# The matmuls of the MLP read their moving operand from two interleaved runs instead of one

## The chip, the cores and the metric

The kernel runs on one core of a Trainium2 chip. The metric is the device time of one execution in microseconds; a profiled execution also gives its span, from the first to the last recorded instruction.

## The reference

Attention with a sigmoid in place of the softmax, for 8 batches of 12 heads, 448 tokens and 64 columns a head, and then an MLP over all 3584 tokens:

```python
scores = scale * q @ k.T - log(S)
attn = sigmoid(scores) @ v            # (8, 12, 448, 64)
x = attn -> (3584 tokens, 768)
h = x @ w_in                          # 768 x 2048
g = relu(h) ** 2
out = g @ w_out                       # 2048 x 768
```

The weights arrive as 64-bit floats and are turned into 32-bit ones on the chip.

## The kernel before

The program has two parts. The first is attention with the preparation of the weights; it runs to about 246 us of the span. The second is the MLP, which works through four groups of tokens, `GROUPS`: three of 1024 tokens (T = 512, twice) and a last one of 512 (T = 256, twice). For each group `gemm1` computes the hidden layer and `gemm2` the output. Both use a block scheme with 7 products in place of 8, over halves of the tokens, of the features and of the weights.

Accuracy comes from splitting. Every 32-bit operand `raw` is split by `split_to` into a high part `hi`, which ScalarE (ACT) writes with a cast to fp32r, and a low part `lo = raw - hi`, which VectorE (DVE) writes. `product` then issues three matmuls for each pair of blocks: high by high, high by low, low by high. The stationary operand `a[:, c]` is a 128 x 128 block of weights, the moving operand `b` a block of T token columns; in the last group's `gemm2` it is the other way round and the moving operand is 384 weight columns wide. TensorE writes each product into one PSUM bank, and sums over blocks there.

In `gemm1`, `run(n, i)` makes product n for weight block i: 3 blocks `c` times 3 passes, so 9 matmuls; 7 products and 8 values of i give 504 matmuls of 512 columns for each of the first three groups. In `gemm2` 7 products, 8 values of i, 3 output blocks e and 3 passes give 504 again. So six stages of 504 matmuls, 3024 in all, have a moving operand of 512 columns (`NS`). In the last group, `gemm1` has operands of 256 columns and some joined ones of 512 columns (`joined_product`, lines 614 and 616), and `gemm2` those of 384.

The moving operands of `gemm1` are made in `x_operands` by `make`: for each of 7 products one call of `split_to` for two blocks together (128 x 1024) and one for the third (128 x 512). Those of `gemm2` are made in `operand_of` by `split`, 28 calls a group of 128 x 1024 each (tiles `o_0h` to `o_3h` and `o_0l` to `o_3l`). The weights are split by `halve_weights`, which calls `split_to` as well (tiles `w`, `w1A` to `w1D`).

The steps of a group follow an order written out by hand (`REST`, and for the first group `LEAD` ahead of it); the `work` lists say behind which step an operand is loaded or split, and parts of the kernel run under `manual_schedule`, in program order. DMAs are issued from SyncE (SP). Attention multiplies plain F32 operands where it forms sums with v (lines 337 and 349): there four matmuls on 64 x 64 tiles of the array stand in a row, two on either half of the partitions, which read two different column runs of the same tile `at`.

Strided access exists already in the preparation of the weights: `convert_upper` (line 158, ACT) and `convert_join` (line 169, DVE) read every second 32-bit word of a tile of 64-bit words, and line 161 (ACT) reads and writes every second word.

Of the kernel before, what the change touches and what calls it, by code (L numbers as in the profile page):

```python
# [30 lines left out]
NS = 512  # L31
# [49 lines left out]
def sigmoid_attention_relu2_mlp(  # L81
# [51 lines left out]
    def op2(name, dtype=F32, n=S):  # L133
        return sb.tile([P, 2, n], dtype, tag="op2", bufs=N2, name=name)

    def op1(name, dtype=F32, n=S):
        return sb.tile([P, n], dtype, tag="op1", bufs=N1, name=name)
# [132 lines left out]
    def raw_of(half, k):  # L270
        if (half, k) not in raw_first:
            raw_first[half, k] = op2(f"x0_{half}{k}", n=NS), op1(f"y0_{half}{k}", n=NS)
        return raw_first[half, k]
# [98 lines left out]
    def split_to(hi, lo, raw, later=None):  # L372
        nc.scalar.copy(out=hi, in_=raw)  # L373
        if later is None:
            nc.vector.tensor_sub(out=lo, in0=raw, in1=hi.bitcast(F32))  # L375
        else:
            later.append(lambda: nc.vector.tensor_sub(out=lo, in0=raw, in1=hi.bitcast(F32)))

    def split(raw, name, new):
        hi, lo = new(name + "h", F32R), new(name + "l", F32R)  # L380
        split_to(hi, lo, raw)
        return hi, lo

    def x_operands(g):

        raw = {}
        t0, T = GROUPS[g]

        def load(n, b, k):
            if g == 0:
                raw[n] = raw_of(b, k)
                return
            r2, r1 = op2(f"x{n}_{g}", n=T), op1(f"y{n}_{g}", n=T)
            src = xd[3 * k : 3 * k + 3, :, t0 + b * T : t0 + (b + 1) * T].rearrange("c p s -> p c s")
            nc.sync.dma_start(out=r2, in_=src[:, 0:2])
            nc.sync.dma_start(out=r1, in_=src[:, 2])
            raw[n] = [r2, r1]

        def sub(n, a, b):
            for o, x, y in zip(raw[n], raw[a], raw[b]):
                nc.vector.tensor_sub(out=o, in0=x, in1=y)

        ops, ys = {}, {}

        def make(product, n, later=None, whole=False):
            if 2 * T > NS:
                y = op2(f"y{n}_{g}", F32R, T)
                h1, l1 = y[:, 0], y[:, 1]  # L410
                h2, l2 = (op2(f"{c}{n}_{g}", F32R, T) for c in ("xh", "xl"))
                ops[product] = [(h2[:, c], l2[:, c], None) for c in range(2)] + [(h1, l1, None)]
            else:
                x = op2(f"xj{n}_{g}", F32R, 2 * T)
                kind, at = SPOT[product]
                if kind not in ys:
                    ys[kind] = op2(f"yj{kind}_{g}", F32R, 2 * T)
                y = ys[kind][:, at]
                (h2, l2), (h1, l1) = ((t[..., :T], t[..., T:]) for t in (x, y))
                ops[product] = [(h2[:, c], l2[:, c], x[:, c]) for c in range(2)] + [(h1, l1, y)]  # L420
            (x2, x1) = raw[n]
            split_to(h2, l2, x2, later)
            if whole:
                later.append(lambda: split_to(h1, l1, x1))
            else:
                split_to(h1, l1, x1, later)

        load("11", 0, 0)
        load("12", 1, 0)
        load("22", 1, 1)  # L430
        load("21", 0, 1)
        raw["t2"] = raw["22"] if g == 0 else [op2(f"xt_{g}", n=T), op1(f"yt_{g}", n=T)]
        raw["t1"], raw["t3"], raw["t4"] = raw["12"], raw["11"], raw["21"]
        return ops, {
            1: lambda *later: make(1, "11", *later),
            2: lambda *later: make(2, "21", *later),
            "t1": lambda: sub("t1", "12", "11"),
            "t2": lambda: sub("t2", "22", "t1"),
            6: lambda *later: make(6, "t2", *later),
            "t3": lambda: sub("t3", "t2", "11"),  # L440
            7: lambda: make(7, "t3"),
            5: lambda: make(5, "t1"),
            3: lambda *later: make(3, "22", *later),
            "t4": lambda: sub("t4", "21", "t2"),
            4: lambda: make(4, "t4"),
        }
# [5 lines left out]
    last = len(pairs) - 1  # L452
    todo = [(m, i) for m in range(2) for i in range(NI) if m == 0 or i not in DEFERRED]
    x, vt, xs, at, pav, xo, f64, w = {}, {}, {}, {}, {}, {}, {}, {}
    ready, stores, later, words = [], [], [], []
# [119 lines left out]
    first = {}  # L575
# [28 lines left out]
    def product(out, w, c, x, first, last):  # L604
        (wh, wl), (xh, xl) = w, x
        for n, (a, b) in enumerate(((wh, xh), (wh, xl), (wl, xh))):
            nc.tensor.matmul(  # L607
                out, a[:, c], b, start=first and n == 0, stop=last and n == 2, skip_group_check=True
            )

    def joined_product(out, w, xs, first):
# [8 lines left out]
    def operand_of(g, raw, name, later=None):  # L620
        T = GROUPS[g][1]
        if 2 * T > NS:
            return (*split(raw, name, lambda *names: op2(*names, T)), None)
        both = op2(name, F32R, 2 * T)
        hi, lo = both[:, :, :T], both[:, :, T:]
        split_to(hi, lo, raw, later)
        return hi, lo, both

    def gemm1(g, ops, weights, between):
# [53 lines left out]
        def run(n, i):  # L683
# [10 lines left out]
            if n in joined:  # L694
                joined_product(out, w, ops[n], n in (1, 7, 2))
            else:
                for c in range(NE):
                    product(out, w, c, ops[n][c][:2], n in (1, 7, 2) and c == 0, c == NE - 1)
# [107 lines left out]
    def gemm2(g, blocks, operands1, weights1, ahead):  # L806
# [50 lines left out]
        for at, n in enumerate(order):  # L857
# [6 lines left out]
            with ExitStack() as fixed:  # L864
                if g == NG - 1 and n == 1:
                    fixed.enter_context(tc.manual_schedule())
                for j in range(NI // 2):
                    if at + 1 < len(order):
                        operand(order[at + 1], j)
                    if n in (4, 3):  # L870
                        ahead((n == 3) * NI // 2 + j)
                    for e in range(parts):
                        for i in (2 * j, 2 * j + 1):
                            w, x = (tuple(t[:, i % 2] for t in of[:2]) for of in (weights[n][j], ops[n][j]))
                            still, moving = (x, w) if turned else (w, x)
                            still = tuple(t.rearrange("p (c m) -> p c m", m=P) for t in still)
                            product(banks[k, e], still, e, moving, n in (1, 7, 2) and i == 0, i == NI - 1)
# [124 lines left out]
```

## Time and profile before

| | |
|---|---|
| median of 3 runs | 1055.15 us (1054.49 to 1055.74) |
| profiled execution, its own time | 1054.99 us |
| its span | 1053.2 us |
| TensorE busy | 1049.0 us, 100% of the span |
| VectorE busy | 802.9 us, 76% |
| ScalarE busy | 657.9 us, 62% |
| mean granted TensorE clock | 1.000 |

The profiled execution spends 1.8 us outside its span. The busy time of TensorE is that of its pipelined matmuls: one matmul is listed with the time from its start to its modelled end, longer than the time after which the next one starts. The pace is read from the chain of work, which lists how many matmuls follow one another in how many microseconds.

### The profile page before, as it was taken

The numbers are of one execution on the slowest core, as the hardware profiler recorded it, in microseconds if no ns is written. First come the engines' busy times: TensorE is split into PE (matmuls) and PEld (weight loads), VectorE is DVE, ScalarE is ACT, GpSimd is POOL, SyncE is SP. The second block draws the span as 40 slices with busy tenths as digits, with TensorE's granted clock in tenths as the row PEclk, the third lists the DMA queues.
The fourth block names the chain that finished last, engine by engine and source line by source line (L and its number), as shares of the span: only waits on it lengthen the run. The fifth ranks groups of instructions, "written<-read, shape, count | busy, mean of one in ns | idle before, by whom it ended". The sixth has DMA issues, their size and how long they took to land.

```text
span 1053.2 us, 16201 instructions
## 1 busy us (share of the span) xinstructions
PE 1049.0 (100%) x6194; PEld 818.3 (78%) x6194; DVE 802.9 (76%) x1024; ACT 657.9 (62%) x917; POOL 72.4 (7%) x42
## 2 busy tenths in 40 slices
PE   9999999999999999999999999999999999999998
PEld 4555555557888888888888888888888888899998
DVE  5999999996777698954555899655555998549994
ACT  7989989986765765634343757344333766248863
POOL 1322232210121000000000000000000000000000
PEclk9999999999999999999999999999999999999999
DMA  9988999964565336544333446442333344557464
GB/s 359 401 296 314 378 388 323 380 239 141 193 217 163 110 109 193 165 132 122 91 90 90 120 128 197 147 151 78 103 98 105 105 142 143 182 172 236 130 189 127
DMA packets 90366, 196.11 MB, mean 186 GB/s; under 512 B 8240, under 2 KB 51504, under 8 KB 90288
## 3 DMA queue, kind: packets, MB, share of 16 engines
q1 hardware_dynamic: 90288, 195.07, 55.9%
q8 instruction: 49, 0.80, 0.3%
q14 instruction: 29, 0.24, 0.1%
HBM read 154.14 MB, written 40.89 MB: 185 GB/s over the span
## 4 chain that ended last, share of the span: by engine, by line
PE 100%; ACT 0%; issue 0%
PE ha L607 22%; PE oa L607 22%; PE ob L607 11%; PE pav L337 11%; PE hb L607 9%; PE sc L305 9%; PE oc L607 5%; PE hc L607 5%; PE sr L322 2%; PE pav L349 2%; PE hb L614 1%; PE hb L616 1%; PE hc L614 1%; PE warm_ps L907 0%; PE hc L616 0%; ACT o L848 0%
## 5 line engine op out<-in xcount | busy, mean ns | idle before, releaser
L373 ACT CAST w<-w 128x768 fp32r<-128x768 f32 x108 | 89.4, 836 | 94.8 <-DMA w<-w 91.5
L375 DVE TENSOR_TENSOR w<-w 128x768 fp32r<-128x768 f32 x108 | 103.0, 956 | 29.3 <-ACT w L373 29.2
L676 ACT COPY s<-ha 128x512 f32<-128x512 f32 (+1 forms) x96 | 51.2, 533 | 118.4 <-PE ha L607 114.3
L290 ACT ACTIVATE at<-sc 128x896 f32<-128x896 f32 x144 | 119.3, 942 | 4.0 <-PE sc L305 3.9
L337 PE MATMUL pav<-at,v 64*64 64x448 f32 x1152 | 118.1, 540 | 0.0
L337 PEld LDWEIGHTS pav<-at,v 64*64 64x64 f32 x1152 | 41.6, 133 | 60.8 <-issue 53.9
L559 DVE TENSOR_TENSOR ql<-x,qh 128x896 fp32r<-128x896 f32 x47 | 72.4, 1581 | 0.0
L172 POOL TENSOR_TENSOR a<-a,f 128x768 int32<-128x768 int32 x26 | 58.2, 2237 | 159.8 <-DVE a L169 89.3
L679 DVE TENSOR_TENSOR g<-hb,s 128x512 f32<-128x512 f32 (+1 forms) x64 | 39.7, 620 | 32.4 <-ACT s L676 25.5
L375 DVE TENSOR_TENSOR w1A<-w1A 128x768 fp32r<-128x768 f32 x24 | 23.0, 957 | 53.6 <-ACT w1A L373 53.4
L305 PE MATMUL sc<-qh 64*128 64x448 f32 x282 | 53.7, 380 | 0.0
L305 PE MATMUL sc<-ql,qh 64*128 64x448 f32 x282 | 51.4, 361 | 0.0
L305 PE MATMUL sc<-qh,ql 64*128 64x448 f32 x282 | 51.4, 361 | 0.0
L373 ACT CAST w1A<-w1A 128x768 fp32r<-128x768 f32 x32 | 26.7, 835 | 32.7 <-DMA w1A<-w 30.0
L607 PE MATMUL oa<-o_0h,w 128*128 128x512 f32 x144 | 46.3, 389 | 0.0
L607 PE MATMUL oa<-o_1h,w 128*128 128x512 f32 x144 | 46.3, 389 | 0.0
L607 PE MATMUL oa<-o_2h,w 128*128 128x512 f32 x144 | 46.3, 389 | 0.0
L607 PE MATMUL oa<-o_3h,w 128*128 128x512 f32 x144 | 46.3, 389 | 0.0
L305 PEld LDWEIGHTS sc<-qh 64*128 64x128 f32 x282 | 26.4, 184 | 18.9 <-PE pav L337 16.2
L659 DVE SCALAR_TENSOR_TENSOR g<-g 128x1024 f32<-128x1024 f32 (+1 forms) x34 | 38.5, 1131 | 1.1
L373 ACT CAST w1C<-w1C 128x768 fp32r<-128x768 f32 x31 | 25.9, 834 | 20.4 <-DMA w1C<-w 20.4
L375 DVE TENSOR_TENSOR w1B<-w1B 128x768 fp32r<-128x768 f32 x23 | 23.0, 1001 | 19.9 <-ACT w1B L373 19.9
(315 smaller groups left out, 2764.8 us busy)
## 6 DMA issues: line engine op xcount, KB each, us to landing
w<-w SPq DMA_DIRECT2D x108, 384.0 KB, 3.3
x<-qk SPq DMA_DIRECT2D x47, 448.0 KB, 6.9
f<-w_in SPq DMA_DIRECT2D x16, 768.0 KB, 8.7
w1A<-w SPq DMA_DIRECT2D x32, 384.0 KB, 3.1
w1B<-w SPq DMA_DIRECT2D x31, 384.0 KB, 3.1
w1C<-w SPq DMA_DIRECT2D x31, 384.0 KB, 3.1
v<-v SPq DMA_DIRECT2D x24, 448.0 KB, 7.7
w<-s SPq DMA_DIRECT2D x26, 384.0 KB, 8.8
```

The lines of the kernel that those rows point to most:

```text
L172: nc.gpsimd.tensor_tensor(out=wb, in0=wb, in1=t.bitcast(I32)[:, :, 0], op=ALU.add)
L290: nc.scalar.activation(at, sc, AF.Sigmoid, bias=NEG_LOG_S, scale=SCALE)
L305: nc.tensor.matmul(sc[t][:, j], x[kp][rows, 1, ks], x[qp][rows, 0], start=(n == 0), stop=(n == len(passes) - 1),)
L322: nc.tensor.matmul(sc[r * KR : (r + 1) * KR, j], x[rows, 1, NT * P :], x[rows, 0], start=True, stop=True)
L337: nc.tensor.matmul(sums[columns, h], vt[rows, n % 2 * NT + t, columns], at[t][rows, j], start=(t == 0 and (n % 2, h) != (1, 1)), stop=(t = ...
L373: nc.scalar.copy(out=hi, in_=raw)
L375: nc.vector.tensor_sub(out=lo, in0=raw, in1=hi.bitcast(F32))
L559: nc.vector.tensor_sub(out=xs[n][1], in0=x[n], in1=xs[n][0].bitcast(F32))
L607: nc.tensor.matmul(out, a[:, c], b, start=first and n == 0, stop=last and n == 2, skip_group_check=True)
L659: nc.vector.scalar_tensor_tensor(out=t, in0=t, scalar=0.0, in1=t, op0=ALU.max, op1=ALU.mult)
L676: nc.scalar.copy(out=s, in_=banks["a", i])
L679: nc.vector.tensor_add(out=to, in0=from_[:, :T], in1=s)
```

## The change

The low and high parts of the moving operands of 512 columns are stored in another order: in each block of 512 tokens the 256 even tokens first, and the 256 odd ones behind them. The casts and subtractions that make these parts read `raw` with a step of two elements (8 bytes) and write the two runs one after the other, through a view with two rows. In `product` a moving operand of 512 columns is read through a view of 256 by 2: even token 0, odd token 0, even token 1, and so on, 1024 bytes to and fro. The order of the columns in the result is as before. The weights, the joined operands and the operands of the last group keep their layout. No instruction is added or removed.

```diff
+    def unwoven(t, order):
+        a = "a " if len(t.shape) > 2 else ""
+        return t.rearrange(f"p {a}({order}) -> p {a}n s", n=2)
+
+    def weave_to(hi, lo, raw, later=None):
+        split_to(unwoven(hi, "n s"), unwoven(lo, "n s"), unwoven(raw, "s n"), later)
+
+    def woven(t):
+        return t.rearrange("p (n s) -> p s n", n=2)
+
     def split(raw, name, new):
         hi, lo = new(name + "h", F32R), new(name + "l", F32R)
-        split_to(hi, lo, raw)
+        weave_to(hi, lo, raw)
         return hi, lo
...
-            split_to(h2, l2, x2, later)
+            to = weave_to if 2 * T > NS else split_to
+            to(h2, l2, x2, later)
             if whole:
-                later.append(lambda: split_to(h1, l1, x1))
+                later.append(lambda: to(h1, l1, x1))
             else:
-                split_to(h1, l1, x1, later)
+                to(h1, l1, x1, later)
...
         for n, (a, b) in enumerate(((wh, xh), (wh, xl), (wl, xh))):
+            moving = woven(b) if b.shape[-1] == NS else b
             nc.tensor.matmul(
-                out, a[:, c], b, start=first and n == 0, stop=last and n == 2, skip_group_check=True
+                out, a[:, c], moving, start=first and n == 0, stop=last and n == 2, skip_group_check=True
             )
```

## Rows read from the trace of the kernel before

**Rows 1.** The page: busy time of TensorE, and its clock in 40 slices.

```profile
PE 1049.0 (100%) x6194; PEld 818.3 (78%) x6194; DVE 802.9 (76%) x1024; ACT 657.9 (62%) x917; POOL 72.4 (7%) x42
...
PEclk9999999999999999999999999999999999999999
```

**Rows 2.** Waits of TensorE: all that the trace shows.

```profile
PE warm_ps L907 <- PEq L988: 0.8, 1, 0.8
```

**Rows 3.** Busy times by stage: attention, six stages of 504 matmuls, the last group.

```profile
core 0: us, PE busy (x) PEld busy (x) DVE busy (x) ACT busy (x) POOL busy (x), PEclk, DMA share, GB/s
0.00:246.32 246.32, 245.55 (x2404) 136.41 (x2405) 221.78 (x301) 216.46 (x280) 58.37 (x30) 1.00 0.90 333
246.32:360.50 114.18, 114.18 (x505) 94.51 (x504) 78.94 (x119) 73.15 (x114) 14.05 (x12) 1.00 0.54 172
...
817.50:931.77 114.27, 114.27 (x507) 94.62 (x506) 91.31 (x103) 64.05 (x84) 0.00 (x0) 1.00 0.47 144
931.77:1053.20 121.43, 117.99 (x768) 114.54 (x767) 97.62 (x160) 78.42 (x140) 0.00 (x0) 1.00 0.56 172
```

**Rows 4.** Chain of work: start, us, matmuls of 512, 256 and 384 columns.

```profile
376.82 16.32 PE oc L607 x72
...
943.48 2.16 PE ha L607 x18
...
999.84 8.32 PE oc L607 x48
```

**Rows 5.** Chain of work in attention: F32 operands of 448 columns, 64 x 64 tiles.

```profile
12.73 0.75 PE pav L349 x8
13.48 2.25 PE pav L337 x24
```

**Rows 6.** Groups of TensorE instructions: the same F32 matmuls, with their count.

```profile
L337 PE MATMUL pav<-at,v 64*64 64x448 f32 x1152 | 118.1, 540 | 0.0
```

**Rows 7.** Groups of ACT by shape: L373 reads in order, L158 every second word.

```profile
L373 ACT CAST w<-w 128x768 fp32r<-128x768 f32 x108 | 89.4, 836 | 94.8 <-DMA w<-w 91.5 <-PE oa L607 3.1
L158 ACT ACTIVATE a<-f 128x768 f32<-128x768 f32 x26 | 25.1, 964 | 0.0
...
L373 ACT CAST w1D<-w1D 128x384 fp32r<-128x384 f32 x32 | 16.4, 513 | 1.6 <-DMA w1D<-w 1.6
...
L158 ACT ACTIVATE b<-fd 128x384 f32<-128x384 f32 x12 | 6.7, 556 | 0.0
```

**Rows 8.** Groups of DVE by shape: L375 reads in order, L169 every second word.

```profile
L375 DVE TENSOR_TENSOR w<-w 128x768 fp32r<-128x768 f32 x108 | 103.0, 956 | 29.3 <-ACT w L373 29.2
...
L169 DVE SCALAR_TENSOR_TENSOR a<-f,a 128x768 int32<-128x768 int32 x26 | 24.9, 959 | 0.9
```

**Rows 9.** Timeline, second group: making o_2 and its first use by TensorE.

```profile
591.55 1.05 ACT L373 CAST o_2h<-g 128x1024 fp32r<-128x1024 f32 x1
...
594.97 1.22 DVE L375 TENSOR_TENSOR o_2l<-g,o_2h 128x1024 fp32r<-128x1024 f32 x1
...
597.24 0.39 PE L607 MATMUL oa<-o_2l,w 128*128 128x512 f32 x1
```

**Rows 10.** Busy times in the first product of the first group's second stage.

```profile
360.50:376.82 16.32, 16.32 (x74) 13.51 (x73) 16.31 (x17) 15.55 (x20) 0.00 (x0) 1.00 0.36 110
```

## The prediction

> **What bounds the kernel now.** The page first: TensorE is busy for 1049.0 of 1053.2 us, at full granted clock in all 40 slices [rows 1]. A busy TensorE can still wait, so the waits come next: in the whole trace TensorE waits once, 0.8 us at the start [rows 2]. Then the stages: six of 504 matmuls take 114.2 to 114.3 us each, busy for the whole stage, clock 1.00 [rows 3]. So whatever one of these matmuls costs more or less goes into the end time with the factor 3024, and what happens on ACT and DVE counts only if TensorE comes to wait for it.
>
> What such a matmul costs is read from the chain of work. 72 matmuls of 512 columns take 16.32 us, so 226.7 ns each; 48 of 384 columns take 8.32 us, so 173.3 ns; 18 of 256 columns take 2.16 us, so 120.0 ns [rows 4]. At 2.4 GHz, the upper of the clock's two levels, which a granted clock of 1.00 is, these are 544, 416 and 288 cycles: the columns plus 32 each time. Read in order, the moving operand therefore comes at one column a cycle, with no cycle lost that grows with its length. All six stages have this pace (504 by 226.7 ns is 114.2 us), so the reads meet nothing that disturbs them. A new read order can win nothing but those 32 cycles.
>
> **The change part by part.**
>
> *The read order.* No instruction is added. What changes is how 3024 matmuls fetch 512 columns: neighbours in the stream were neighbours in memory, 4 bytes apart; now each lies 1024 bytes from the one before. No matmul of this kernel reads like that, so I bound the price. Below: one column a cycle as today, 0 ns; a gain is limited to the 32 cycles, 13.3 ns. Above, the slowest stream of columns here is that of plain F32 operands in attention: 24 instructions of 448 columns take 2.25 us [rows 5], and as four tiles of the array run side by side (front: four matmuls on 64 x 64 tiles stand in a row), a set of four takes 375 ns or 900 cycles, 2.0 cycles a column. The code makes 576 calls at that line and the page counts 1152 instructions [rows 6], so a whole F32 matmul comes to 4.0 cycles a column. My bounds are thus 1 and 4 cycles a column, with a row at 2.0 between them.
>
> I take 2 cycles a column. A fp32r stream moves 4 bytes a cycle at 2.4 GHz on every partition, and the simplest way to hold that rate is to fetch several neighbours in one access. If it is done that way, the smallest such unit is a pair, and the new order breaks every pair: two accesses where there was one. That is an estimate from the bounds; no row shows the size of the unit. The sum: 2 by 512 plus 32 are 1056 cycles, 440.0 ns, 213.3 ns more than today; by 3024 it is 645.1 us. At 4 cycles a column it is 2080 cycles, 866.7 ns, 640.0 ns more and 1935 us in all.
>
> There is a rule that speaks against this read order in words. The Trainium skill, page SBUF — State Buffer (section "Door 1: The DMA port swizzle"), says that SBUF has 16-byte lines, that at least two consecutive accesses must fall on one line for full bandwidth, and that each step to a new line pays a penalty. In the old order four fp32 columns share a line, in the new one none do, so by that rule all 3024 matmuls slow down, by an amount that the page does not give; without it they stay at 226.7 ns. The trace before agrees in part: ACT, reading every second word, so two to a line, takes 964 ns in place of 836 for 768 elements [rows 7], where the rule would have it free, and DVE pays nothing [rows 8].
>
> *The casts on ACT.* A group has 7 products of two casts in its first stage and 28 casts in its second, 42; three groups have 126, of 1024 or 512 elements, which now read with a step of 8 bytes. The nearest rows: 964 against 836 ns for 768 elements, 556 against 513 for 384 [rows 7] (line 158 is another function, so part of it may not be the step). That is 0.11 to 0.17 ns an element, so 0.12 to 0.17 us for a cast of 1024, and no more than 21 us over the MLP, while ACT is idle for 41 to 50 us in the first and last of these stages alone [rows 3]. The cover for a single cast: o_2h ends at 592.60 and the subtraction behind it starts at 594.97 [rows 9], 2.4 us later. I cost it at nothing. If the cover were gone, each of the 126 would cost at most its 0.17 us.
>
> *The subtractions on DVE.* Also 126, with one input at a step of 8 bytes. Line 169, with such an input, takes 959 ns for 768 elements, the plain subtraction 956 [rows 8]. So nothing, and that matters: DVE is busy for 16.31 of 16.32 us where it is fullest [rows 10], and o_2l is written 1.05 us ahead of its first reader [rows 9]. 0.2 us more for each would eat that lead after five operands, and TensorE would wait. Were TensorE slower, both engines would gain time.
>
> *Everything else.* The writes stay runs of 256 elements, the loads are untouched, attention's 246 us and the last group's 121 us [rows 3] have no woven matmul. Each sum starts from the profiled execution, 1054.99 us (1053.2 of span and 1.8 around it), 0.16 us below the median of the runs, 1055.15. 1055.0 + 645.1 = 1700.
>
> **The rivals.**
>
> *The order of reads is free* (not slower; the change then does nothing to the time). Place: the fetch of a moving operand. If the memory serves any 4 bytes a cycle, the pace stays 544 cycles, and the time 1055. For it: the four tiles of attention read two different runs of one tile from the same partitions, 448 columns each in 375 ns [rows 5], so 896 elements in 900 cycles from two places, if they run side by side as the pace says. Against it: those may be two streams, each in order, and not one that jumps; and ACT's reads do feel a step [rows 7]. It decides as soon as one stream may jump every cycle without loss.
>
> *A mild penalty.* If jumping costs TensorE what a step costs ACT, 8 to 15% of the time [rows 7], a matmul takes 19 to 35 ns more, and 3024 of them 58 to 105 us: 1113 to 1160. For it: it is the only price of a stride in the trace. Against it: a step of two words leaves neighbours closer than a jump of 1024 bytes.
>
> *Four cycles a column or near it*: 1055 + 1935 = 2990. It comes if a fetch brings four columns and each jump loses three. For it: F32 operands run at that rate in sum [rows 5, 6]. Against it: there the rate comes from two instructions, not from the fetch.
>
> *A gain.* If part of the 32 cycles belongs to opening one run and two runs hide it, at most 13.3 ns by 3024, 40 us: 1015. Nothing in the trace ties them to the read order; they are the same for 256, 384 and 512 columns.
>
> **How the numbers follow.** Half rate 0.36; free 0.31; a mild penalty, with all between it and half rate, 0.13; beyond half rate 0.13; a gain 0.07. The likeliest gives the time, 1700; its own range is 1690 to 1745 (up to 2.07 cycles a column, 15 ns a matmul or 45 us in all; a little below for a pace not quite at 2). The range that leaves out the gain and everything beyond half rate, 0.20 together, is 1050 to 1745; it is wide because cases of both signs hold most of the chance. A measurement of this kernel can tell about 0.2% from no change: faster 0.07, same 0.31, slower 0.62.
>
> **What would show it.** The chain of work of the stage that starts near 360 us: 72 matmuls in 31.7 us for half rate, 16.3 if reads are free, 17.7 to 18.8 for the mild case, 62.4 at four cycles. The matmuls of 256 and 384 columns keep 120.0 and 173.3 ns in every case. ACT's casts of 1024 should go from 1.05 to about 1.2 us, DVE's subtractions stay at 1.22; under half rate both should show more idle time, waiting for TensorE. The prediction is wrong if the pace stays at 226.7 ns, or if TensorE shows waits for o_l or xl tiles. A granted clock below 1.00 in these stages would be a cost that I have not put in.

## The result and the profile after

The changed kernel takes 1026.88 us (median of 4 runs, 1026.30 to 1027.27) against 1054.86 for the kernel before beside it: ratio 0.9733, 95% interval 0.9716 to 0.975. It is 28 us faster, where 645 us more were forecast. The span went from 1053.2 to 1025.5 us.

The page shows less TensorE time and more on ACT and DVE, to set beside [rows 1]:

```profile
PE 1018.4 (99%) x6194; PEld 821.8 (80%) x6194; DVE 834.4 (81%) x1024; ACT 711.3 (69%) x917; POOL 72.3 (7%) x42
```

The pace is in the chain of work (start, us, what):

```profile
372.17 15.54 PE oc L619 x72
...
980.38 8.32 PE oa L619 x48
```

72 matmuls of 512 columns take 15.54 us in place of 16.32 [rows 4]: 215.8 ns or 518 cycles each, columns plus 6 in place of columns plus 32. The matmuls of 384 columns, which the change leaves alone, keep their 8.32 us for 48. 3024 by 10.8 ns are 32.8 us, but the span lost only 27.7. The busy times by stage show where the other 5 went:

```profile
246.34:356.42 110.08, 109.39 (x505) 95.29 (x506) 81.21 (x120) 78.72 (x112) 13.96 (x12) 1.00 0.57 178
...
465.41:575.87 110.46, 109.42 (x505) 95.01 (x505) 64.76 (x75) 51.76 (x76) 0.00 (x0) 1.00 0.37 109
575.87:684.65 108.78, 108.78 (x506) 95.26 (x505) 103.01 (x98) 77.76 (x76) 0.00 (x0) 1.00 0.48 151
```

The columns are those of [rows 3]. 504 by 215.8 ns are 108.78 us: the second stage of a group keeps that, the first stages take 1.3 to 1.8 us more, and TensorE is idle in them, which it was not before. Its waits are these (engine, us in total, times, longest):

```profile
PE ha L619 <- ACT s L688: 2.2, 3, 0.8
...
PE hb L619 <- DVE w1D L375: 0.6, 2, 0.3
```

The larger wait comes once in each first stage: TensorE waits for `s`, a copy of its sums out of PSUM, which stands on ACT behind casts of tokens. In the second group these took 1.56 us (xh) and 0.81 (y) in place of 1.05 and 0.62. The smaller wait comes at the end of the second and the third first stage, as the chain of work there shows:

```profile
567.56 1.96 PE ha L619 x9
...
570.02 1.58 ACT o_0h L373
571.60 0.42 ACT w1D L373
...
572.03 1.55 DVE o_0l L375
573.58 0.47 DVE w1D L375
...
574.10 1.78 PE hb L619 x7
```

TensorE's last product of the stage waits for w1D's low part, which stands on DVE behind o_0l, which waits for a cast of 1.58 us on ACT. Both are longer than before, and so are instructions that the change does not touch (groups by shape, mean ns in the second figure):

```profile
L373 ACT CAST o_1h<-g 128x1024 fp32r<-128x1024 f32 x18 | 29.3, 1625 | 0.6 <-DVE g L843 0.5
...
L158 ACT ACTIVATE b<-fd 128x384 f32<-128x384 f32 x12 | 8.5, 708 | 0.0
...
L375 DVE TENSOR_TENSOR o_0l<-g,o_0h 128x1024 fp32r<-128x1024 f32 x18 | 28.1, 1562 | 1.3 <-ACT o_0h L373 1.3
...
L169 DVE SCALAR_TENSOR_TENSOR b<-fd,b 128x384 int32<-128x384 int32 x12 | 8.1, 671 | 0.4
```

The cast of 1024 elements went from 1.05 [rows 9] to 1.6 us, the subtraction from 1.22 to 1.55. Line 158, which converts weights and has no part in the change, went from 556 ns [rows 7] to 708. So there were two questions: which part of the change makes a matmul 26 cycles shorter, and what lengthens strided reads on two other engines.

### The profile page after: what moved, and what is told of

Same layout as the page of the kernel before. It is cut to its first block, busy times and chain, and to the rows that moved or that the text cites. A ratio compares the mean times of both kernels' runs of the same rounds, so it can differ in the third digit from the quotient of the medians.

```text
span 1025.5 us, 16201 instructions
## 1 busy us (share of the span) xinstructions
PE 1018.4 (99%) x6194; PEld 821.8 (80%) x6194; DVE 834.4 (81%) x1024; ACT 711.3 (69%) x917; POOL 72.3 (7%) x42
## 4 chain that ended last, share of the span: by engine, by line
PE 95%; ACT 2%; DMA 1%; issue 0%; DVE 0%; SPq 0%; ACTq 0%
PE oa L619 21%; PE ha L619 20%; PE pav L337 11%; PE ob L619 11%; PE sc L305 9%; PE hb L619 8%; PE oc L619 5%; PE hc L619 4%; PE sr L322 2%; PE pav L349 2%; PE hb L626 1%; DMA w1A<-w 1%; DMA w1D<-w 1%; PE hb L628 1%; PE hc L626 1%
## 5 line engine op out<-in xcount | busy, mean ns | idle before, releaser
L375 DVE TENSOR_TENSOR w<-w 128x768 fp32r<-128x768 f32 x108 | 103.5, 963 | 20.2 <-ACT w L373 20.2
L373 ACT CAST w<-w 128x768 fp32r<-128x768 f32 x108 | 90.4, 848 | 41.6 <-DMA w<-w 41.6
L375 DVE TENSOR_TENSOR w1A<-w1A 128x768 fp32r<-128x768 f32 x24 | 22.9, 955 | 39.8 <-ACT w1A L373 39.6
L373 ACT CAST w1A<-w1A 128x768 fp32r<-128x768 f32 x32 | 26.7, 835 | 29.4 <-DMA w1A<-w 27.9
L355 ACT COPY xo<-pav 128x448 f32<-128x448 f32 x48 | 25.6, 533 | 19.6 <-PE pav L349 10.9
L566 DVE CAST qh<-x 128x896 fp32r<-128x896 f32 x47 | 32.5, 729 | 6.8 <-DMA x<-qk 6.8
```

The costliest lines, as they stand in the source:

```text
L566: nc.vector.tensor_copy(out=xs[n][0], in_=x[n])
```

## The experiments

**Only the reads.** Storage and casts of before; the output copies put the tokens back.

```diff
+            moving = woven(b) if b.shape[-1] == NS else b
...
+                return t if turned else t.rearrange(f"p {order} -> p s m", m=4)
...
+            o_ = rows(o, "(m s)")
```

> The storage and the casts are those of before; only the moving operands of 512 columns are read from the two halves in turn, so columns come out in another order after each stage, and the 36 output copies of the first three groups write their tile with a step of 128 words to put the tokens back. Theory (the read order alone ends each matmul 26 cycles earlier, and it costs the other engines nothing if they read in order): 72 matmuls in 15.54 us, casts of 1024 back at 1.05 us and subtractions at 1.22, no waits of TensorE, 1054.9 - 32.8 = 1022 us. Rival (the gain needs operands that were written as two runs): 72 matmuls in 16.32 us, 1055. On the conversions of weights that fall into the MLP (lines 158, 161, 169, 128 x 384, which no change touches): if TensorE's jumping reads slow strided reads of other engines, they take 0.71, 0.72 and 0.67 us as in the changed kernel; if not, 0.56, 0.55 and 0.56 as before.

Measured: 1023.12 us, ratio 0.9696 (0.9682 to 0.9711), and TensorE waits for nothing but the start.

```profile
370.47 15.54 PE oc L611 x72
```

```profile
L373 ACT CAST o_1h<-g 128x1024 fp32r<-128x1024 f32 x18 | 18.8, 1042 | 1.4 <-DVE g L835 1.4
...
L158 ACT ACTIVATE b<-fd 128x384 f32<-128x384 f32 x12 | 8.6, 717 | 0.0
```

The first fence is the chain of work, the second the groups by shape. The read order alone carries the whole gain. Casts that read in order are not slowed, but line 158, which reads every second word, is, although here neither it nor any cast was changed. So the slowing comes from how TensorE reads, or from the stepped output copies, the other thing that this kernel changes; the run on distance below has no such copies, and there the same jump gives the same 0.70 us.

**Only the storage.** The other half of the change: woven operands, read in order.

```diff
-            moving = woven(b) if b.shape[-1] == NS else b
+            moving = b
```

> The operands are stored as even tokens, then odd ones, but read in order (tokens come out in another order, which is left so). Theory (pace belongs to the read order): 72 matmuls in 16.32 us, and no gain: 1055 to 1057. Rival: 15.54 us and about 1027. On the price of the casts: if the step of 8 bytes costs it by itself, casts of 1024 take 1.60 us and subtractions 1.55 as in the changed kernel; if it is TensorE's jumping reads that slow them, they take about 1.05 to 1.2 and 1.22 here.

Measured: 1055.08 us, ratio 1.0002 (0.9993 to 1.0012); 72 matmuls take 16.32 us again:

```profile
376.87 16.32 PE oc L619 x72
```

The step of 8 bytes by itself costs a cast 0.09 us and a subtraction nothing:

```profile
L373 ACT CAST o_1h<-g 128x1024 fp32r<-128x1024 f32 x18 | 20.4, 1133 | 0.0
...
L375 DVE TENSOR_TENSOR o_1l<-g,o_1h 128x1024 fp32r<-128x1024 f32 x18 | 22.0, 1224 | 2.2 <-ACT o_1h L373 2.1
```

**Read orders compared.** One kernel, 21 products, each with another order, `how`. The sums mix tokens.

```diff
+    def in_turn(t, n, k):
+        return t.rearrange("p (n s k) -> p s n k", n=n, k=k) if k > 1 else t.rearrange("p (n s) -> p s n", n=n)
...
+            if isinstance(how, tuple):
+                moving = in_turn(b, *how)
```

> Storage of before; each of the 21 products of the three second stages reads its moving operand in another way (sums then mix tokens, and some products fill only 64 rows or 256 columns). Read: us of 72 matmuls, 16.32 for 544 cycles, 15.54 for 518. First group: one word each from 2, 4, 8, 16, 32, 64, 128 runs in turn. Second: two runs, 2, 4, 8, 16, 32, 64, 128 words at a time. Third: 256 runs (steps of two words), every word twice, 64 weight columns, two halves one after the other, 64 weight columns with two runs in turn, 256 columns, 256 columns from two runs in turn. Theory 1 (the 26 cycles are lost where a stream goes on within or to the next 16-byte line): 15.54 for all first-group orders up to 128 runs, and for two runs while 1 or 2 words are taken at a time; 16.32 from 4 words on and for 256 runs. Theory 2 (any pattern with a second dimension is served another way): 15.54 for all of them but the two halves one after the other. Theory 3 (the 26 cycles are a clash with the weight load that runs at the same time): 64 weight columns read in order lose about half, 531 cycles or 15.9 us, and with two runs 518 as with 128. 256 columns: 288 cycles, 8.64 us, in order, and 262 cycles, 7.86 us, in turn, under all three.

The chain of work of the first group's second stage, in the order 2, 4, 8, 16, 32, 64 and 128 runs:

```profile
360.09 15.54 PE oa L627 x72
375.63 20.39 PE oc L627 x72
396.02 35.07 PE oa L627 x72
431.09 31.32 PE ob L627 x72
462.41 31.20 PE oa L627 x72
493.61 31.04 PE ob L627 x72
524.65 33.22 PE oa L627 x72
```

Two more rows of the same chain, two runs taken two words at a time and a step of two words:

```profile
672.21 24.00 PE oa L627 x72
...
913.02 32.63 PE oa L627 x72
```

All of it in cycles a matmul (us by 2400 over 72):

| order of 512 columns | cycles |
|---|---|
| one word each from 2, 4, 8, 16, 32, 64, 128 runs | 518, 680, 1169, 1044, 1040, 1035, 1107 |
| every second word, then the others (256 runs) | 1088 |
| two runs, 2, 4, 8, 16, 32, 64, 128 words at a time | 800, 600, 584, 576, 568, 545, 544 |
| two halves one after the other | 545 |
| every word twice | 518 |
| 64 weight columns: in order; two runs in turn | 552; 518 |

None of the three theories stands. The first wanted 518 up to 128 runs, the second 518 for any second dimension, the third a smaller loss with half the weight columns; it is no smaller. What is seen: two runs, one word each, cost only 6 cycles over their columns; one word each from 8 or more runs costs 2 cycles a column or a little more, as the prediction had it, and a step of two words does so as well; four runs, and two runs taken several words at a time, lie between. 256 columns take 288 cycles in order and 268 in turn (72 between 1018.11 and 1026.14 us), where the expectation had 262.

**Runs close together.** The pattern suggested theory L, stated in the expectation; it was tested with two runs inside small blocks, where shape and distance can be told apart.

```diff
+    def near(t, s, n=2):
+        return t.rearrange("p (m n s) -> p m s n", n=n, s=s)
...
+            if isinstance(how, int):
+                moving = near(b, how)
```

> Storage of before. Second stage of the first group: two runs in turn inside blocks of 4, 8, 16, 32, 64, 128, 256 words (runs of 2, 4, 8, 16, 32, 64, 128 words). Second group: even words twice each; 128 words four times each; in turn but for the low part, which is read in order; in turn but for the first pass; four runs of 4 words in turn; 384 columns in order; 384 columns in turn. First stage of the first group and the fp32r scores of attention: runs of 4 words in turn (outputs mix tokens). Theory L (columns are fetched two at a time, the even and the odd ones each through a 16-byte line of their own; a line serves as many columns of its stream as follow on it: four cost nothing, two cost the 26 cycles, one halves the rate): us of 72 matmuls 16.32 for runs of 2 and 15.54 from 4 words up; even words twice 16.32; four times 15.54; four runs of 4 about 20.4 as for four far runs; 384 columns 12.48 and 11.70. Theory S (what counts is the shape, two steps inside one, however near): 15.54 for runs of 2 and for even words twice as well. If the 26 cycles belong to the matmul that reads in order and not to its neighbours, the two mixed products take 15.80; if a neighbour is enough, up to 16.06. First stage: 9 matmuls in 1.94 us in place of 2.04 under both. Scores: a pair of 448 columns takes 454 cycles or 189 ns in place of 480 or 200. If a jump of 16 bytes disturbs the strided reads of ACT as a jump of 1024 does, line 158 takes 0.71 us for 384 elements, else 0.56.

The chain of work; the first three rows are runs of 2, 4 and 8 words (those of 16 to 128 are like the last), then even words twice, four times, and the two mixed products, four runs of 4, and 384 columns in order and in turn:

```profile
352.07 16.39 PE oa L632 x72
368.46 15.54 PE oc L632 x72
384.00 15.54 PE oa L632 x72
...
576.01 16.32 PE oa L632 x72
592.33 15.54 PE oc L632 x72
607.87 16.00 PE oa L632 x72
623.87 15.88 PE ob L632 x72
639.75 19.34 PE oa L632 x72
659.08 12.51 PE ob L632 x72
671.59 11.70 PE oa L632 x72
```

What theory L says of the 26 cycles came out: runs of 2 words lose them, runs of 4 do not; even words twice, of the same shape, lose them, four times does not. The shape theory falls. As a rule for all orders theory L is not shown. By its last clause, that one column to a line halves the rate, four runs taken one word each and two runs taken two words at a time should have cost about 1088 cycles as well, since both streams change their line at every column there; they took 680 (645 when the four runs are near) and 800. Where it gives 544, for two far runs taken 4 to 64 words at a time, 600 to 545 were measured. And the mixed products lost more than the matmuls read in order alone should (16.00 and 15.88 for 15.80), so the matmul next to one read in order loses something too, or the one in order loses more than 26 there. Line 158 took 558 ns in this kernel: a jump of 16 bytes does not disturb it. In attention, sets of 36 score matmuls in the stretch before the MLP took 3.60 to 3.74 us, not the 3.4 of the expected 189 ns a pair; before they took 3.83, so a pair did lose up to 13 ns.

**The change with near runs.** One number of the change is another: blocks of 8 tokens.

```diff
-        a = "a " if len(t.shape) > 2 else ""
-        return t.rearrange(f"p {a}({order}) -> p {a}n s", n=2)
+        a, am = ("a ", "(a m)") if len(t.shape) > 2 else ("", "m")
+        return t.rearrange(f"p {a}(m {order}) -> p {am} n s", n=2, s=4)
...
-        return t.rearrange("p (n s) -> p s n", n=2)
+        return t.rearrange("p (m n s) -> p m s n", n=2, s=4)
```

> The change as it is, casts and all, with one number changed: the two runs lie 16 bytes apart, in blocks of 8 tokens (4 even ones, then 4 odd ones), in place of 1024 bytes. Theory (the jump of 1024 bytes slows strided reads of ACT and DVE, and their longer casts and subtractions make TensorE wait; a jump of 16 bytes does neither): pace 15.54 us for 72, casts of 1024 at 1.14 us as with plain reads of TensorE, subtractions 1.22, line 158 0.56 us, no waits of TensorE, 1022 us: 4 to 5 less than the changed kernel. Rival (the two engines are slowed by TensorE's faster pace or by the two-run order itself, near or far): casts 1.60, subtractions 1.55, 1027.

Measured: 1022.37 us, ratio 0.9694 (0.9678 to 0.971), 4.5 us less than the change as it was; no waits of TensorE after its start. Casts take 1144 ns, subtractions 1214, line 158 556, as expected (the chain of work, then the groups by shape):

```profile
370.26 15.54 PE oc L619 x72
```

```profile
L373 ACT CAST o_1h<-g 128x1024 fp32r<-128x1024 f32 x18 | 20.6, 1144 | 1.2 <-DVE g L843 1.2
```

**How far is far.** The distance is changed from step to step of the first group's first stage, while weights are being converted.

```diff
+    RUNS = {6: 4, 9: 16, 12: 64, 15: 256, 17: 8, 20: 32, 23: 128, 26: 0, 28: 256, 31: 64, 34: 128, 37: 32, 40: 0}
...
...
-                out, a[:, c], b, start=first and n == 0, stop=last and n == 2, skip_group_check=True
+                out, a[:, c], b.rearrange("p (m n s) -> p m s n", n=2, s=s) if s else b, start=first and n == 0, stop=last and n == 2, skip_group_check=True
```

> Storage of before; only the first stage of the first group reads in turn, with a distance between the two runs that changes from step to step (16, 64, 256, 1024, 32, 128, 512 bytes, then in order, 1024, 256, 512, 128 bytes, in order; outputs mix tokens). Read: the twelve conversions of 128 x 384 on ACT (lines 158 and 161) and on DVE (line 169), one after the other, each with the distance that TensorE jumps at that time. Theory (a jump slows strided reads if it is far): 0.56 us at 16 bytes and in order, 0.71 at 1024, and a distance between them from which it rises. Rival (it was the permanent use of one order, or the output copies, and not the jump at that time): the same time for all twelve.

The timeline of ACT, at jumps of 16, 64, 128, 512 and 256 bytes in this order; in order, at 299.87, it took 0.56:

```profile
262.31 0.56 ACT L158 ACTIVATE b<-fd 128x384 f32<-128x384 f32 x1
...
267.41 0.56 ACT L158 ACTIVATE b<-fd 128x384 f32<-128x384 f32 x1
...
287.82 0.57 ACT L158 ACTIVATE b<-fd 128x384 f32<-128x384 f32 x1
...
292.67 0.70 ACT L158 ACTIVATE b<-fd 128x384 f32<-128x384 f32 x1
...
308.82 0.74 ACT L158 ACTIVATE b<-fd 128x384 f32<-128x384 f32 x1
```

Up to 128 bytes nothing is slowed; at 256, 512 and 1024 bytes (0.70 at 304.55) strided reads are. DVE's line 169 agrees: 0.56 us at 32, 64 and 128 bytes, 0.65 to 0.69 at 256 and more. Distances that are no power of two were not tried.

**The rest of the matmuls.** Three kernels extend near reads. The first two keep storage as it was and put the order back where results leave PSUM, `near_all` in attention too:

```diff
-            nc.vector.tensor_add(out=to, in0=from_[:, :T], in1=s)
...
+                to = near(to)
+                nc.vector.tensor_add(out=to, in0=turned_once(from_[:, :T]), in1=turned_once(s))
```

> Storage and casts of before; all matmuls of the MLP, the last group's 768 too, read their moving operand in turn from two runs of 4 words, 16 bytes apart; the output copies, and in the last group the instructions that take the first stage out of PSUM, write with a step that puts the tokens or features back. Theory L: 26 cycles or 10.8 ns less for each of 3792 matmuls, 41.1 us: 1014. If the joined matmuls and those of 256 and 384 columns did not gain: 1022. If the stepped writes became late: above 1016, with waits of TensorE on tiles that they write.

> As the kernel with near runs in the whole MLP, and the scores of attention read their queries in the same order; put_x writes the tokens back in order. Theory L: 423 pairs of score matmuls at 10.8 ns, 4.6 us less, 1009. Rival (attention is held by ACT, DVE and DMA nearly as much as by TensorE): the gain is swallowed by waits, 1012 to 1015.

Measured: 1023.68 us, ratio 0.97 (0.9686 to 0.9715), and 1027.87 us, ratio 0.9747 (0.9731 to 0.9763). Both expectations missed. In the first, the last group's matmuls did become shorter, but the stepped writes on DVE grew from 424 to 636 ns, and DVE became the bound there (waits of TensorE: engine, us in total, times, longest):

```profile
PE ha L619 <- DVE w1A L377: 3.3, 3, 1.7
```

In the second, attention ended 4.4 us later than in the first (249.85 against 245.44 us, start of the MLP on the chain). Its sets of 36 fp32r score matmuls went from 3.83 us to 3.60 where nothing held them. Against that its trace shows two losses, which no run took apart. The plain F32 score matmuls of the last 64 keys (line 322), which this kernel reads in turn as well, went from 0.75 us for 8 to 0.94 or 0.95, some 4.6 us over their 24 sets; and the additions that write the tokens back went from 617 to 989 ns.

The third weaves the last group's token operands when they are cast, so that no PSUM copy of its first stage writes with a step:

```diff
+            to = weave_to if 2 * T > NS else weave_halves_to
...
+            nc.tensor.matmul(out, wh[:, c], woven_halves(both, 2), ...)
```

> The kernel with runs of 4 words in blocks of 8 tokens, and the last group too: its token operands are stored as even and odd tokens of a block of 256 (14 casts and subtractions with a step of 8 bytes) and read in turn, and its weight operands of 384 columns are read in turn from runs of 4 words, 14 output copies putting the features back. Nothing that reads PSUM in the last group's first stage writes with a step. Theory (the near version of the whole MLP lost its gain to the stepped writes alone, which made DVE late): 768 matmuls at 10.8 ns, 8.3 us less than the 1022.4 of the three groups alone, and up to 0.4 us back in the last copy: 1014 to 1015, no waits of TensorE. Rival (the last group is held by DVE and ACT anyway once TensorE is faster): 1018 to 1022, with waits on casts of weights.

Measured: 1016.51 us, ratio 0.9639 (0.9622 to 0.9655), the fastest of all, 2 us above the expectation. The last group's second stage has its full gain, 48 matmuls of 384 columns in 7.80 us. Its first has not: matmuls of 256 columns take 18 in 2.01 us, 268 cycles each, so they lose 20 cycles and not 26, about 0.9 us less in all for the 360 of them; and the stage ran partly along DVE and ACT, where TensorE waited 1.1 us.

```profile
902.63 2.01 PE ha L632 x18
...
963.83 7.80 PE oc L632 x48
```

## Why the prediction was wrong

**What bounds the kernel** was read rightly: TensorE's pace times 3024. So was the bound of a gain, "nothing but those 32 cycles": 26 of them went.

**The step that failed** is "I take 2 cycles a column", with its reason that the new order breaks every pair: it forecast 1056 cycles or 440.0 ns for a matmul, and 518 cycles or 215.8 ns were measured, 10.8 ns less than before in place of 213.3 more. Such a price exists, but for other orders: a step of two words costs 1088 cycles, and 8 to 128 runs cost 1035 to 1169. If TensorE takes columns in pairs, the two members of a pair need not be neighbours. Theory L, as far as the scans bear it out, says what must be near: each second column to the one two places before it. The woven order puts those next to each other, four to a line of 16 bytes, where the plain order has two. The Trainium skill's rule for lines of 16 bytes (page SBUF — State Buffer, section "Door 1: The DMA port swizzle"), which spoke against the change, comes nearer to the runs when read for the even and the odd columns apart; as it stands it is contradicted from both sides here: every access of the woven order goes to a new line and the matmuls got shorter, and a step of two words, two to a line, halved the rate.

**The gain as a rival** had 0.07, because nothing tied the 32 cycles to the read order: they are the same for 256, 384 and 512 columns. That was true of the rows and a poor reason. A constant cost can still belong to one way of reading, when all rows read that way. The free reads that attention's rows pointed to, two streams from two places [rows 5], were nearer to what came, though no run shows that the two have one cause.

**The casts** were priced at 0.12 to 0.17 us more, the subtractions at nothing. Alone that is about right: 0.09 and nothing (only the storage). Together with TensorE's jumps of 1024 bytes it was 0.55 and 0.33. The prediction named the consequence, 0.2 us more on DVE and TensorE waits, but by way of o_l and xl tiles, and the trace after shows no wait of TensorE for either. The waits came in the first stages, for the most part by ACT, whose longer casts the prediction had costed at nothing: 2.2 us for `s` and 0.6 for w1D. With what TensorE loses around each wait it was 4.5 us, the difference between jumps of 1024 and of 16 bytes. What it missed is that two edits, each costed by rows where the other was absent, are not costed together.

**The rest** held: attention, the last group and the granted clock of 1.00 did not change.

Three things stay open: why the plain order costs 26 cycles once in a matmul, and not in proportion to its columns (20 at 256 columns); why four runs lose so much less than eight; and why strided reads of ACT and DVE get longer when TensorE jumps by 256 bytes or more.

## What to carry to other kernels

When TensorE is the bound and a matmul takes a constant number of cycles more than its columns, try another read order of the moving operand before taking the constant as given; two runs of four 32-bit words read in turn, 16 bytes apart, slowed no strided read of the other engines here, and the step in the casts cost 0.1 us a cast. This was seen for fp32r operands; plain F32 ones got slower. Put the order right where data is written into SBUF by an engine with time to spare, not in copies out of PSUM that are already the next bound. When a change touches how two engines use the same memory, look in the trace after for unchanged instructions that became longer: they tell of the interaction.

## What the runs showed of the hardware that was not expected

- fp32r matmuls of the MLP take their columns plus 32 cycles when the moving operand is read in order. When two runs of four or more words are read in turn, it is plus 6 for 512 and 384 columns (518 for 544, 390 for 416) and plus 12 for 256 (268 for 288). Half the weight columns change nothing of the 518.
- Plain F32 score matmuls of 448 columns got longer when read in turn from runs of four words: 8 in 0.94 us in place of 0.75.
- A moving operand with a step of 8 bytes takes 1088 cycles for 512 columns.
- While TensorE's reads jump by 256 bytes or more, reads with a step of 8 bytes take longer: on ACT 0.69 to 0.76 us in place of 0.55 for 384 elements, on DVE 0.65 to 0.69 in place of 0.56. Reads in order keep their time, 1042 ns for a cast of 1024.
